# Two k loads moved ahead of DMA transposes, and two weight subtractions moved from VectorE to GpSimd, in a fused attention and maxout kernel

## Chip, cores and metric

The kernel runs on one core of a Trainium2 chip. The metric is device time in microseconds (us) of one execution, the median of several runs; a profiled execution gives the trace. Engines are written as in the profile: PE (TensorE; PEld is its weight loads), DVE (VectorE), ACT (ScalarE), POOL (GpSimd), SP (SyncE, which here issues nearly all DMAs; "SPq" is its queue).

## What is computed

Soft-capped attention over 8 batches of 12 heads (448 positions of 64 elements), then a layer of two first matrices with a maximum between them:

```python
scores = scale * np.matmul(q, k.transpose(0, 1, 3, 2))
scores = cap * np.tanh(scores / cap)
scores = scores - np.max(scores, axis=-1, keepdims=True)
attn = np.exp(scores)
attn = attn / (np.sum(attn, axis=-1, keepdims=True) + 1e-09)
...
h1 = x @ w1                # x: 3584 x 768, the heads side by side
h2 = x @ w2
g = np.maximum(h1, h2)
return (g @ w_out).astype(np.float32)
```

The kernel uses max(h1, h2) = h2 + relu(h1 - h2). It subtracts w2 from w1 once (wd_sb, eight 128-column blocks of x @ (w1 - w2) go through a relu), and multiplies w2 by w_out once (wm_sb), so the output is x @ wm + relu(x @ wd) @ w_out.

## The kernel before

**Units.** Two heads are a pair; there are 48 pairs, 6 in a batch. A group is 3 pairs (L = 3), numbered from 0 in the code, so that there are groups 0 to 15. A step t is 2 pairs (NQ = 24 steps): step t uses pairs 2t and 2t + 1, and pair i belongs to group i // 3. So group 4 is first used by pair 12, the scores of step 6, part 0, and group 5 by pair 15, the scores of step 7, part 1.

**Way of a group.** `load` (L117) issues from SP the DMAs of k, q or v of a group into f32 tiles `kr`, `qr`, `vr`, two buffers each, so a load of group g needs the casts of group g - 2 to be done. From group 2 on a load of k is three DMAs (main, L129, 576 KB, and two of the left-over rows, L142, 48 KB each), one of q two (L129, 576 KB, and L136, 96 KB), one of v three like k. `cast` (L147) turns them to bf16 on POOL: k in L185 and two of L197, q in L185 and L190, v in L164 and two of L169. `cross` (L290) then issues one DMA transpose from SP (L292), from `kqf` to `qkT`, for groups from 2 on; groups 0 and 1 are transposed by PE (`transposes`, L273). `scores` (L302) multiplies from `qkT` (L318, or L315 for the left-over rows of both pairs, part 2) and applies tanh on ACT (L319), out of two `s` buffers and one `v` buffer of PSUM; `ex` (L321) exponentiates on ACT (L324). `add` (L331) sums exponentials on DVE from step 4 on (`esum`, L342 to L346), `total` (L352) makes the row sums and their inverse, `values` (L373) multiplies with v (L381, L387), `normalize` (L400, DVE) writes `xT`.

**Filler.** `moe(b)` (L406) is a generator of the matmuls of one batch: blocks f = 0 to 7 of six matmuls each (L414) with a relu on DVE (L419), then output tiles (L429, L432) with a copy on DVE (L435) and DMAs out. Two PSUM buffers (`mm`) alternate. `F(n)` (L460) emits the next n matmuls of the oldest generator, so PE's order is written out by hand: scores, filler, scores, filler, row sums, values. What is left at the end is emitted at once (L697).

**Weights.** `load_w1` (L228) loads w1 in chunks c = 0 to 5 and halves (columns 0 to 511 and 512 to 1023); `subtract(c, half, engine)` (L234, L236) makes wd_sb. Chunks 0 to 3 lie in tiles named `osb`, 4 and 5 in one named `xT`. The second halves are needed by the blocks f = 4 to 7 of `moe(0)`.

**Order.** Every engine works through its own instructions in the order in which the program emits them, and SP likewise: an issue that has to wait for a semaphore holds up all that are behind it. The schedule is a list written out by hand (L505 to L648) and a loop over the steps from 3 on (L650). `todo[i]` holds loads that `extra(i)` (L494) issues in step i // 2, `crosses[t]` the group that step t transposes (before `extra(2t)`), `casts[t]` the casts at the end of step t, held back by a small copy to `mark` on POOL (L691) that waits for the inverse of that step. Groups from 4 on are planned by L485 to L492; here the lists that matter are todo[4] = k and q of group 4, todo[6] = k and q of group 5, todo[8] = v of group 4, todo[5] empty, crosses[4] = 4, crosses[5] = 5, and casts[3] (moved ahead of the loop, L627) and casts[4] = k and q of groups 4 and 5. L647 moves group 5's loads from step 3 to step 4, behind the transposes of group 4.

Of the kernel before, what the change touches and what calls it, by code (L numbers as in the profile page):

```python
# [10 lines left out]
def kernel(  # L11
# [11 lines left out]
    nc = tc.nc  # L23
# [75 lines left out]
    def half(b):  # L99
        return slice(0, 64) if b % 2 == 0 else slice(64, P)  # L100

    def rows(t, b, h0, h1):

        return t[b, h0:h1, :, :].rearrange("h (r j) d -> (h r) (j d)", j=R7)
# [4 lines left out]
    def raw_of(g, what):  # L109
        if (g, what) not in raw:  # L110
            raw[g, what] = raw_tile(what)
        t = raw[g, what]
        m = t[:, : 2 * L * NJ * D].rearrange("p (h c) -> p h c", c=NJ * D)
        l = t[:, 2 * L * NJ * D :].rearrange("p (h d) -> p h d", d=D)
        return t, m, l

    def load(g, what, n0=0, n1=L, parts=("main", "left")):  # L117
        b, p = divmod(g * L, NP)
        h0, h1 = 2 * (p + n0), 2 * (p + n1)
        src = {"k": k, "q": q, "v": v}[what]  # L120
        t, m, l = raw_of(g, what)
        if g < NT:
            nc.sync.dma_start(
                out=t[:, n0 * S : n1 * S].rearrange("p (n c) -> p n c", c=S),
                in_=rows(src, b, h0, h1).rearrange("(n p) c -> p n c", p=P),
            )
            return
        if "main" in parts:
            nc.sync.dma_start(  # L129
                out=m[:, 2 * n0 : 2 * n1, :],  # L130
                in_=src[b, h0:h1, 0 : NJ * P, :].rearrange("h (p j) d -> p h (j d)", j=NJ),
            )
        if "left" not in parts:
            return
        if what == "q":
            nc.sync.dma_start(  # L136
                out=l[half(b), 2 * n0 : 2 * n1, :],
                in_=src[b, h0:h1, NJ * P : S, :].rearrange("h p d -> p h d"),
            )
        else:  # L140
            for par in range(2):
                nc.sync.dma_start(  # L142
                    out=l[64 * par : 64 * par + 64, n0:n1, :],
                    in_=src[b, h0 + par : h1 : 2, NJ * P : S, :].rearrange("h p d -> p h d"),
                )
# [88 lines left out]
    def subtract(c, part, eng):  # L234
        cs = slice(part * (DF // 2), (part + 1) * (DF // 2))
        eng.tensor_sub(wd_sb[:, c, cs], w1_in[c][:, cs], w2b[part][:, c, :])  # L236
# [31 lines left out]
    def qkT_of(g):  # L268
        if g not in qkT:
            qkT[g] = stage.tile([P, L, 8, P], bf16, name="qkT")  # L270
        return qkT[g]
# [18 lines left out]
    def cross(g, n0=0, n1=L):  # L290

        nc.sync.dma_start_transpose(  # L292
            out=qkT_of(g)[:, n0:n1].rearrange("p n j c -> p (n j) c"),
            in_=kqf[g % 2][:, n0:n1].rearrange("p n j c -> p (n j c)"),
        )
# [6 lines left out]
    def scores(t, p, last=None, js=None):  # L302

        if (t, p) not in tanh:
            tanh[t, p] = att.tile([P, 2 * NJ, S], bf16, name="tanh")
        for j in js or range(NJ if p < 2 else 1):
            s = two_banks(last if last and j == NJ - 1 else s_psum)
            for m in range(2):
                i = 2 * t + (p if p < 2 else m)
                g = i // L  # L310
                k0 = qkT[g][:, i % L, :, :].rearrange("p j c -> p (j c)")
                o = Q0 + (64 * (i // NP % 2) if g >= NT else 0)
                qTn = k0[:, o : o + S]
                if p == 2:
                    nc.tensor.matmul(s[:, m, :S], k0[:, 3 * P : 4 * P], qTn)  # L315
                else:
                    r = slice(64 * m, 64 * m + 64)
                    nc.tensor.matmul(s[:, m, :S], k0[r, j * P : (j + 1) * P], qTn[r, :])  # L318
            nc.scalar.activation(tanh[t, p][:, 2 * j : 2 * j + 2, :], s[:, :, :S], AF.Tanh, scale=scale / cap)  # L319

    def ex(t, p):  # L321
        n = 2 * NJ if p < 2 else 2
        expo[t, p] = att.tile([P, n, S], bf16, name=f"expo{p}", bufs=2)
        nc.scalar.activation(expo[t, p], tanh[t, p][:, 0:n, :], AF.Exp, scale=float(cap))  # L324
# [6 lines left out]
    def add(t, ab, step):  # L331

        if t < NS or t >= NQ:
            return
        if t not in esum:
            esum[t] = att.tile([P, 4, S], bf16, name="esum")
        d = esum[t][:, 2 * ab : 2 * ab + 2, :]
        if step == 2:

            r = slice(64 * ab, 64 * ab + 64)  # L340
            d = esum[t][r, ab::2, :]
            nc.vector.tensor_add(d, d, expo[t, 2][r, :, :])  # L342
        elif step == 0:
            nc.vector.tensor_add(d, e_of(t, ab, 0), e_of(t, ab, 1))  # L344
        else:
            nc.vector.tensor_add(d, d, e_of(t, ab, 2))  # L346
# [5 lines left out]
    def total(t):  # L352

        ss = two_banks(s_psum)[:, 0, :]
        if t < NS:
            for j in range(NJ):
                for ab, h, r in HEADS:
                    nc.tensor.matmul(
                        ss[r, :S], ones[:, :32], e_of(t, ab, j)[:, h, :], start=(j == 0), stop=False
                    )  # L360
            for ab, h, r in HEADS:
                nc.tensor.matmul(ss[r, :S], ones2[:, h, :32], expo[t, 2][:, ab, :], start=False, stop=True)
        else:
            for ab, h, r in HEADS:
                nc.tensor.matmul(ss[r, :S], ones[:, :32], esum[t][:, 2 * ab + h, :], start=True, stop=True)  # L365
        st = att.tile([P, NB, 32], f32, name="st", bufs=1)
        nc.vector.transpose(st.rearrange("p b c -> p (b c)"), ss[:, :S])  # L367
        rs = att.tile([P, NB, 1], f32, name="rs", bufs=2)
        nc.vector.reciprocal(rs, st[:, :, 0:1])
        inv[t] = att.tile([P, S], f32, name="inv", bufs=2)  # L370
        nc.vector.transpose(inv[t].rearrange("p (b c) -> p b c", c=32), rs.to_broadcast([P, NB, 32]))  # L371
# [28 lines left out]
    def normalize(t, ps):  # L400
        for u in range(2):
            nc.vector.tensor_mul(x_of(t, u), ps[:, u, :S], inv[t])  # L402
# [57 lines left out]
    def F(n):  # L460
        rate[1] += n * rate[0]
        while rate[1] >= 1 and fill_q:
            g = fill_q[0]
            if g is not rate[2]:
                rate[2] = g
                next(g)
            rate[1] -= 1
            try:
                next(g)
            except StopIteration:  # L470
                fill_q.pop(0)
        if not fill_q:
            rate[1] = 0.0
# [4 lines left out]
    todo = [[] for _ in range(N)]  # L478
# [15 lines left out]
    def extra(i):  # L494
        for f, a in todo[i]:
            f(*a)
# [56 lines left out]
    def cast_kq(g, n0, n1):  # L553
        for what in ("k", "q"):
            cast(nc.gpsimd, g, what, n0, n1)
# [46 lines left out]
    total(0)  # L602
    transposes(5)
    cast_kq(3, 0, 1)
    for c in range(3):
        subtract(c, 1, nc.gpsimd)
    F(8)
    scores(2, 1, js=(0, 1))
# [8 lines left out]
    load_mains(3, 1, 3)  # L617
    load(2, "v")
    cast_kq(3, 1, 3)
    cross(3, 1, 3)  # L620
    extra(4)
    extra(5)
    load(3, "v")
    total(1)
    normalize(1, values(1))
# [18 lines left out]
    scores(3, 2)  # L644
    ex(3, 1)
    F(14)
    todo[8] = todo[6] + todo[8]  # L647
    todo[6] = []  # L648

    for t in range(3, NQ):  # L650
        i = 2 * t
        more = t + 1 < NQ
        if more:
            scores(t + 1, 0, v_psum)
        ex(t, 2)
        if t == 3:
            subtract(3, 1, nc.vector)
        F(6)
        if t in crosses:
            cross(crosses[t])  # L660
        if t == 3:
            subtract(4, 1, nc.vector)
            cast(nc.gpsimd, 3, "v")
        extra(i)
        F(2)
        add(t, 0, 0)
        F(3)
        if t == 3:
            subtract(5, 1, nc.vector)
        add(t, 0, 1)  # L670
        F(3)
        add(t, 1, 0)
        F(2)
        if more:
            scores(t + 1, 1, v_psum)
            ex(t + 1, 0)
        F(3)
        add(t, 1, 1)
        F(7)
        add(t, 0, 2)  # L680
        F(4)
        add(t, 1, 2)
        extra(i + 1)
        F(8)
        if more:
            scores(t + 1, 2)
            ex(t + 1, 1)
        total(t)
        normalize(t, values(t))
        if casts[t]:  # L690
            nc.gpsimd.tensor_copy(mark, inv[t][:1, :1])  # L691
            for g, what in casts[t]:
                cast(nc.gpsimd, g, what)
        if t % 3 == 2:
            fill_q.append(moe(t // 3))
        F(9)
# [34 lines left out]
```

## Time and profile before

| what | value |
|---|---|
| median of 4 runs | 340.93 us (340.53 to 341.13) |
| profiled execution: its own time, its span | 343.09 us, 340.8 us |
| PE busy | 325.2 us, 95% |
| ACT busy | 278.3 us, 82% |
| DVE, POOL busy | 232.1 us (68%), 111.6 us (33%) |
| chain that ended last, by engine | PE 71%, DMA 15%, POOL 4%, SPq 4%, DVE 3% |
| DMA | 61.78 MB, 181 GB/s over the span |

The span goes from the first to the last instruction; all positions below are us from its start. A line of a timeline gives start, duration, engine, source line, operation, output <- inputs with partitions x elements, and how often in a row; in square brackets stand how long the engine was idle just before it and what ended that. The ends of matmuls are modelled. SP's issues count as the time in which SP was busy issuing, not that of the transfer.

### The profile page before, as it was taken

The numbers are of one execution on the slowest core, as the hardware profiler recorded it, in microseconds if no ns is written. First come the engines' busy times: TensorE is split into PE (matmuls) and PEld (weight loads), VectorE is DVE, ScalarE is ACT, GpSimd is POOL, SyncE is SP. The second block draws the span as 40 slices with busy tenths as digits, with TensorE's granted clock in tenths as the row PEclk, the third lists the DMA queues.
The fourth block names the chain that finished last, engine by engine and source line by source line (L and its number), as shares of the span: only waits on it lengthen the run. The fifth ranks groups of instructions, "written<-read, shape, count | busy, mean of one in ns | idle before, by whom it ended". The sixth has DMA issues, their size and how long they took to land.

```text
span 340.8 us, 6876 instructions
## 1 busy us (share of the span) xinstructions
PE 325.2 (95%) x2722; PEld 163.7 (48%) x2722; DVE 232.1 (68%) x416; ACT 278.3 (82%) x243; POOL 111.6 (33%) x194
## 2 busy tenths in 40 slices
PE   4899998989899999999999999999999999999995
PEld 2555443444444554455445544445445554555563
DVE  5446966597687678776787668776776767874321
ACT  4999999897989999899989999899989999900000
POOL 8345685272424404412421441243144130000000
PEclk9999999999999999999999999999999999999999
DMA  7999999859999999577967599749955920012022
GB/s 227 188 238 273 293 252 272 191 146 230 221 238 280 214 224 288 141 160 157 306 174 160 94 241 312 160 136 236 291 117 147 220 83 15 0 48 92 2 92 92
DMA packets 106239, 61.78 MB, mean 181 GB/s; under 512 B 62816, under 2 KB 101216, under 8 KB 106208
## 3 DMA queue, kind: packets, MB, share of 16 engines
q1 hardware_dynamic: 102336, 58.21, 67.3%
q0 software_dynamic: 3872, 3.15, 6.0%
q8 instruction: 21, 0.34, 0.4%
q14 instruction: 10, 0.08, 0.1%
HBM read 42.47 MB, written 11.01 MB: 157 GB/s over the span
## 4 chain that ended last, share of the span: by engine, by line
PE 71%; DMA 15%; POOL 4%; SPq 4%; DVE 3%; issue 2%; POOLq 0%; DVEq 0%
PE mm L432 20%; PE mm L414 18%; PE mm L429 15%; DMA vr<-in_v_dram 6%; PE v L381 6%; PE s L318 5%; DMA kr<-in_moe_w_out_dram 2%; DMA gT<-in_moe_w_dram 2%; PE s L315 2%; DMA qkT<-kqf 2%; PE v L318 2%; PE v L387 2%; DMA xT<-in_moe_w_dram 2%; PE s L365 2%; DMA osb<-in_moe_w_dram 1%
## 5 line engine op out<-in xcount | busy, mean ns | idle before, releaser
L324 ACT ACTIVATE expo<-tanh 128x2688 bf16<-128x2688 bf16 (+1 forms) x72 | 140.3, 1950 | 0.2
L319 ACT ACTIVATE tanh<-s 128x896 bf16<-128x896 f32 x123 | 107.4, 915 | 16.6 <-PE s L318 13.3
L432 PE MATMUL mm<-wo_sb,gT 128*128 128x384 bf16 x448 | 85.8, 327 | 0.0
L414 PE MATMUL mm<-xT,wd_sb 128*128 128x448 bf16 x384 | 78.2, 353 | 2.2 <-DVE gT L419 1.9
L429 PE MATMUL mm<-wm_sb,xT 128*128 128x384 bf16 x336 | 66.1, 327 | 0.0
L435 DVE COPY osb<-mm 128x384 f32<-128x384 f32 x56 | 31.1, 555 | 44.9 <-PE mm L432 44.5
L432 PEld LDWEIGHTS <-gT 128*128 128x128 bf16 x448 | 42.4, 98 | 34.4 <-issue 8.2
L414 PEld LDWEIGHTS <-wd_sb 128*128 128x128 bf16 x384 | 35.9, 98 | 40.6 <-issue 10.0
L419 DVE TENSOR_SCALAR gT<-mm 128x448 bf16<-128x448 f32 x64 | 39.5, 622 | 18.8 <-PE mm L414 18.6
L429 PEld LDWEIGHTS <-xT 128*128 128x128 bf16 x336 | 31.6, 98 | 26.2 <-issue 6.5
L319 ACT ACTIVATE tanh<-v 128x896 bf16<-128x896 f32 x45 | 41.5, 923 | 0.0
L691 POOL COPY mark<-inv 1x1 f32<-1x1 f32 x17 | 3.0, 177 | 115.8 <-DVE inv L371 92.5
L381 PE MATMUL v<-expo,vp 128*32 128x448 bf16 x576 | 36.0, 353 | 0.0
L318 PE MATMUL s<-qkT 64*128 64x448 bf16 x198 | 28.5, 363 | 2.9 <-DVE qkT L288 1.5
L402 DVE TENSOR_TENSOR xT<-v,inv 128x448 bf16<-128x448 f32 x48 | 27.8, 620 | 2.6 <-PE v L387 0.3
L342 DVE TENSOR_TENSOR esum<-esum,expo 64x896 bf16<-64x896 bf16 x40 | 27.1, 677 | 1.2
L367 DVE STREAM_TRANSPOSE st<-s 128x448 f32<-128x448 f32 x24 | 15.6, 650 | 16.5 <-PE s L365 12.5
L346 DVE TENSOR_TENSOR esum<-esum,expo 128x896 bf16<-128x896 bf16 x40 | 26.2, 654 | 0.8
L344 DVE TENSOR_TENSOR esum<-expo 128x896 bf16<-128x896 bf16 x40 | 26.2, 656 | 0.0
L318 PEld LDWEIGHTS <-qkT 64*128 64x128 bf16 x288 | 10.4, 95 | 25.0 <-issue 16.3
L185 POOL CAST kqf<-kr 128x1152 bf16<-128x1152 f32 (+2 forms) x17 | 16.6, 976 | 14.3 <-DMA kr<-in_k_dram 14.3
L381 PEld LDWEIGHTS <-vp 128*32 128x32 bf16 x576 | 15.6, 97 | 10.2 <-DVE vl L161 0.4
(68 smaller groups left out, 267.1 us busy)
## 6 DMA issues: line engine op xcount, KB each, us to landing
vr<-in_v_dram SPq DMA_DIRECT2D x14, 576.0 KB, 5.0
out_dram<-osb SPq DMA_DIRECT2D x20, 384.0 KB, 4.0
kr<-in_k_dram SPq DMA_DIRECT2D x12, 576.0 KB, 6.8
qr<-in_q_dram SPq DMA_DIRECT2D x12, 576.0 KB, 7.5
out_dram<-osb SPq DMA_DIRECT2D x16, 192.0 KB, 3.7
osb<-in_moe_w_dram SPq DMA_DIRECT2D x8, 256.0 KB, 5.0
gT<-in_moe_w_dram POOLq DMA_DIRECT2D x12, 128.0 KB, 9.5
wo_sb<-in_moe_w_out_dram POOLq DMA_DIRECT2D x4, 384.0 KB, 8.9
```

The costliest lines, as they stand in the source:

```text
L318: nc.tensor.matmul(s[:, m, :S], k0[r, j * P : (j + 1) * P], qTn[r, :])
L319: nc.scalar.activation(tanh[t, p][:, 2 * j : 2 * j + 2, :], s[:, :, :S], AF.Tanh, scale=scale / cap)
L324: nc.scalar.activation(expo[t, p], tanh[t, p][:, 0:n, :], AF.Exp, scale=float(cap))
L342: nc.vector.tensor_add(d, d, expo[t, 2][r, :, :])
L344: nc.vector.tensor_add(d, e_of(t, ab, 0), e_of(t, ab, 1))
L381: nc.tensor.matmul(ps[r, :S], vp[g % 2][:, 2 * n + h, j, u::2], e_of(t, ab, j)[:, h, :], start=(j == 0), stop=False,)
L402: nc.vector.tensor_mul(x_of(t, u), ps[:, u, :S], inv[t])
L414: nc.tensor.matmul(ps[:, :S], wd_sb[:, c, f * P : (f + 1) * P], x[:, c, cs], start=(c == 0), stop=(c == KC - 1))
L419: nc.vector.tensor_relu(g[f // FH][:, f % FH, cs], ps[:, :S])
L429: nc.tensor.matmul(ps[:, : DM // 2], x[:, c, ts], wm_sb[:, c, hs], start=(c == 0), stop=False)
L432: nc.tensor.matmul(ps[:, : DM // 2], g[f // FH][:, f % FH, ts], wo_sb[:, f, hs], start=False, stop=(f == FC - 1))
L435: nc.vector.tensor_copy(osb[:, hs], ps[:, : DM // 2])
```

## The change

Of the six second-half subtractions, five are now on POOL ahead of step 3's loop, where three were; chunks 3 and 4 leave DVE, chunk 5 stays there. The load of k of group 4 is issued in front of the transposes of group 3 (its pairs 1 and 2), that of q behind them; the load of v of group 3 still follows. Of group 5, the load of k goes back to step 3, so that it is issued behind v of group 3 and in front of the transposes of group 4; q stays behind them, in step 4. (A count of groups from 1, instead of the code's from 0, makes these loads those of groups 5 and 6 and the transposes those of groups 4 and 5.)

```diff
@@ -602,7 +602,7 @@
     total(0)
     transposes(5)
     cast_kq(3, 0, 1)
-    for c in range(3):
+    for c in range(5):
         subtract(c, 1, nc.gpsimd)
     F(8)
     scores(2, 1, js=(0, 1))
@@ -617,9 +617,9 @@
     load_mains(3, 1, 3)
     load(2, "v")
     cast_kq(3, 1, 3)
+    load(4, "k")
     cross(3, 1, 3)
-    extra(4)
-    extra(5)
+    load(4, "q")
     load(3, "v")
     total(1)
     normalize(1, values(1))
@@ -644,8 +644,8 @@
     scores(3, 2)
     ex(3, 1)
     F(14)
-    todo[8] = todo[6] + todo[8]
-    todo[6] = []
+    todo[8] = todo[6][1:] + todo[8]
+    todo[6] = todo[6][:1]
 
     for t in range(3, NQ):
         i = 2 * t
@@ -653,13 +653,10 @@
         if more:
             scores(t + 1, 0, v_psum)
         ex(t, 2)
-        if t == 3:
-            subtract(3, 1, nc.vector)
         F(6)
         if t in crosses:
             cross(crosses[t])
         if t == 3:
-            subtract(4, 1, nc.vector)
             cast(nc.gpsimd, 3, "v")
         extra(i)
         F(2)
```

## The prediction

> **What bounds the kernel now.** I read the page's busy shares, then busy time by stage, then the timelines of the single engines around the edited lines. [...]TensorE's clock is granted in full in every slice, so no part of the sum hangs on it. Busy time by stage (length, then busy us of PE, weight loads, DVE, ACT, POOL; clock, DMA share, GB/s):
>
> ```profile
> 52.90:58.40 5.50, 4.29 (x28) 1.69 (x22) 4.29 (x6) 5.21 (x6) 2.92 (x3) 1.00 1.13 239
> 58.40:67.00 8.60, 8.60 (x83) 4.26 (x82) 5.19 (x9) 7.91 (x6) 3.61 (x8) 1.00 0.86 202
> 67.00:80.50 13.50, 11.93 (x98) 6.05 (x97) 11.24 (x16) 11.49 (x10) 7.21 (x9) 1.00 0.74 167
> 80.50:96.50 16.00, 14.67 (x109) 6.74 (x109) 11.22 (x21) 14.86 (x14) 5.71 (x9) 1.00 1.03 228
> 96.50:141.00 44.50, 44.10 (x365) 21.67 (x366) 33.69 (x60) 42.57 (x36) 15.64 (x26) 1.00 1.01 250
> 141.00:293.00 152.00, 151.62 (x1216) 74.28 (x1216) 112.85 (x202) 145.52 (x128) 43.54 (x73) 1.00 0.68 170
> ```
>
> From 96.5 to 293 us PE idles 0.4 of 44.5 and 0.4 of 152 us: what comes earlier at 96.5 is passed on to the end. Ahead of that it idles 1.2, 1.6 and 1.3 us in the first, third and fourth stretch, 4.1 us together: the most that this change can win. ACT stands close behind (14.86 of 16.00). PE's timeline names the places:
>
> ```profile
> 56.12 1.67 PE L414 MATMUL mm<-xT,wd_sb 128*128 128x448 bf16 x8 [1.21 <-DVE gT L419]
> ...
> 76.53 0.37 PE L365 MATMUL s<-esum,ones 128*32 128x448 bf16 x3 [1.05 <-DVE esum L342]
> ...
> 80.52 0.55 PE L318 MATMUL s<-qkT 64*128 64x448 bf16 x4 [0.53 <-DMA qkT<-kqf]
> ...
> 96.57 0.55 PE L318 MATMUL s<-qkT 64*128 64x448 bf16 x4 [0.52 <-DMA qkT<-kqf]
> ```
>
> The first is a PSUM buffer of the MoE filler, late because DVE sat in front of its relu. The third and fourth are transposes landing late: of group 4 (first used at 80.52) and group 5 (96.57). DVE, then POOL, then SP's queue:
>
> ```profile
> 54.05 1.49 DVE L236 TENSOR_TENSOR wd_sb<-osb,gT 128x512 bf16<-128x512 f32 x1 [1.47 <-DMA osb<-in_moe_w_dram]
> 55.46 0.61 DVE L419 TENSOR_SCALAR gT<-mm 128x448 bf16<-128x448 f32 x1
> ```
>
> ```profile
> 52.72 2.27 POOL L236 TENSOR_TENSOR wd_sb<-osb,gT 128x512 bf16<-128x512 f32 x2 [1.08 <-DMA osb<-in_moe_w_dram]
> 57.57 0.92 POOL L185 CAST kqf<-kr 128x768 bf16<-128x768 f32 x1 [2.58 <-DMA kr<-in_k_dram]
> ...
> 69.77 1.15 POOL L185 CAST kqf<-kr 128x1152 bf16<-128x1152 f32 x1 [7.11 <-DMA kr<-in_k_dram]
> ...
> 72.45 1.63 POOL L185 CAST kqf<-qr 128x1152 bf16<-128x1152 f32 x1 [0.17 <-DMA qr<-in_q_dram]
> ```
>
> ```profile
> 60.45 1.95 SPq L292 DMA_TRANSPOSE qkT<-kqf  x1
> 62.44 0.99 SPq L129 DMA_DIRECT2D kr<-in_k_dram  x1
> ...
> 64.80 0.60 SPq L129 DMA_DIRECT2D qr<-in_q_dram  x1
> ...
> 74.94 3.64 SPq L292 DMA_TRANSPOSE qkT<-kqf  x1
> ...
> 90.06 4.51 SPq L292 DMA_TRANSPOSE qkT<-kqf  x1
> ```
>
> SP finishes issuing at 56.5, then stands until 60.45 for POOL's casts of group 3; all of group 4's loads stand behind that. It stands again from 70.4 to 74.94 for group 4's casts, with group 5's loads behind; DMA moves 45 and 3 GB/s in 72 to 74 and 74 to 76.
>
> **Part 1: two subtractions from DVE to POOL.** Removed from DVE: the wait of 1.47 for w1's chunk 3, its subtraction of 1.49, and one of 0.67 (chunk 4). The relu of 55.46 then runs when its matmuls end, about 53.6, done by 54.3; PE's 8 matmuls start at 54.9 (end of the 8 before) and not at 56.12. The next scores need two s buffers (ACT's tanh of 54.57 and 55.4 frees them by 56.3) and the v buffer, freed by the tanh of 56.18 at 57.10. So PE resumes filler at 57.10 + 0.35 = 57.45 and not at 58.41: gain **0.96**, not 1.21.
>
> Added to POOL: 2 of 1.15 us, between 54.99 and its next cast at 57.57, which waits 2.58 us for a DMA. Chunk 4's data have landed by 55.3, so POOL runs to 57.29 and delays nothing, with 0.28 us to spare. Behind it stand the casts of group 3 and SP's transposes of them. A rule speaks against this move: the Trainium skill, "GPSIMD Engine Reference", section 4.1, gives elementwise two-input work to VectorE, GpSimd being about 2 times slower. The rows say 1.15 against 0.67 us, 1.7 times. By the rule the pair takes 2.7 us and overruns the gap by 0.1; by the rows it fits. I take the rows: cost 0. Upper bound: DVE's 1.49 beside POOL's subtractions shows a collision costing 0.8; a pair stretched so is 0.5 late, and the transposes with it. It is not below nothing, since the casts still wait for the same DMA. The filler's fifth block, the first to use the second half of wd_sb, needs chunk 3 at about 57.7 (ready 56.2) and chunk 4 at 57.9 (ready 57.3): no wait, with 0.6 us to spare. Chunk 5 stays on DVE.
>
> **Part 2: load of k, group 4, ahead of the transposes of group 3.** Three issues, 0.99 + 1.27 = 2.26 us, go into SP's stand at 56.5 and end at 58.8, ahead of 60.45: no cost to SP while POOL's casts hold it there, up to 2.26 us if they did not. Its buffer was read for the last time at 48.7: no wait. q's group 4 then follows the transposes at 62.4, not 64.8, and v's group 3 likewise: 2.4 us earlier. The bytes are the price: 576 + 2 x 48 = 672 KB at 246 GB/s (62 to 72) is 2.8 us of DMA, in a stretch full until 60 and nearly empty (0.26) until 62. The Trainium skill, "DMA: Bandwidth & Descriptors", section "Queues, rings and completion order", says that each DMA engine consumes one queue's descriptors in ring order, which speaks against both loads here: by that, whatever of k is left stands wholly ahead of the transposes. Before, these landed 4.3 us after issue, at 64.75, and the scores start at 67.00. By the rule at worst 64.75 + 2.8 = 67.5; by the rows, 6.5 us to landing at 90.06 behind v and outputs against 5.5 at 74.94 with nothing ahead, +1.0: 65.8. I take 65.8, since k's load has two nearly empty us to drain in. With part 1 the scores want them at 66.04: cost 0, bounds 0 and 1.5.
>
> **Part 3: group 4's transposes.** k is cast before q comes. q lands 7.5 us after issue as before: 69.9 and not 72.3. Casts of q (before 1.63 and 0.89, ending 74.9) end between 71.6 and 72.4. Transposes: +5.5 as at 74.94, so 77.5; k of group 5, now issued behind v at 68 to 70.4 (in SP's second stand, with 1.2 us to spare; its buffer was last read at 59.1), puts its 2.8 us ahead of them. In ring order from 65.8 come q, v, k at 2.8 each, to 74.2, and then 4 us of transposes (the 76 to 80 stretch): about 78.6. By the rows' +1.0: 78.5. The two agree; without backlog 77.1, with one twice as long 80.
>
> PE's own side: from 66.04, 11.93 us of work, plus the DVE wait at 76.53 of 0 to 1.05: 77.97 to 79.02. That wait comes from esum additions that took 1.56 (one) and 3.31 us (two) beside POOL's casts, against 0.65 for one alone; with k's casts gone from that stage some collisions go, q's and v's remain. I take the middle. ACT: the gaps at 58.20 and 67.47 shrink with PE, and from 66.5 its 11.5 us end at 78.0. The latest of the three: PE's scores at about 78.8, not 80.52: gain **1.72**, part 1 included.
>
> **Part 4: group 5.** k, landed by 75, is cast at once when POOL's gate opens (before: 4.58 us of waiting). q goes out behind the transposes of group 4, about 76 and not 80.58, v of group 4 behind it; q's casts end near 83.5 and not 90.03. Transposes are out by 84 to 86 and land by 92. The scores of 96.57 want them at 94.3: the 0.52 goes. ACT has 15.0 us between these two tanh, PE 15.5: PE sets it. Gain **0.5**.
>
> **Sum.** 1.72 + 0.52 = 2.24, say 2.3 us with the parts rounded. Behind, group 6's transposes landed at 115.1 for scores at 116.80; their gate is a DVE result of the same stage, and their loads go out earlier, so they move along. The profiled execution took 343.09 (span 340.8 and 2.3 around it): I expect a span of 338.5, an execution of 340.8. The median of runs, 340.93, is 2.2 below the profiled one for the same work: 340.93 - 2.3 = **338.6**.
>
> **Rivals.**
> A (0.60), as worked out, with group 4's scores between 78.0 and 79.6: gain 1.4 to 3.0, 337.9 to 339.5.
> B (0.15), the DVE wait at 76.53 goes entirely and transposes come in 77.1: PE and ACT both allow 78.0, and 0.5 + 0.2 behind it: gain 3.2 to 3.7, 337.2 to 337.7. For it: two of six casts leave the stage. Against: q's and v's are the later ones.
> C (0.15), a wait takes the place of the removed one: the k loads take back ahead of the transposes what the early issue gives, and group 4's land at 80 as before. Then part 1's gain ends in a longer wait there; left are 0.5 to 0.9: 340.2. For it: DMA is full from 62 to 72. Against: it is empty from 72 to 76.
> D (0.10), slower: k of group 5 shares the engines with q of group 4, which lands at 72.3 as before, or later; casts end at 74.9 and the transposes need 6.5, not 5.5: 81.4. It decides as soon as they are issued after about 74.5: then the scores lose 0.9, more than the 0.5 left at 96.57. Price 0.4 to 1.2: 341.7.
>
> Two runs of this kernel can be told apart from about 0.2% (0.7 us). Faster by more than that: A, B and nearly half of C, 0.82; the rest of C and a little of D, 0.09; slower, 0.09. For 8 in 10 the range goes from B's lower end to C's middle: 337.2 to 340.4.
>
> **What would show it.** Right: no DMA wait in DVE's L236 near 54; POOL's second pair done by 57.6; transposes of group 3 landed before their scores (no wait at 66); group 4's issued near 72; no DMA wait of PE at group 5's first scores, which start near 94.3; idle unchanged behind. Wrong: PE waiting for qkT at 66, group 4's transposes issued later than 74, an esum wait over 1 us, or ACT gaps kept while PE's shrink.

## The result, and the profile after

| | before | after |
|---|---|---|
| median of runs | 341.59 us (63 runs, 339.59 to 343.18) | 340.56 us (44 runs, 339.33 to 342.59) |
| profiled execution, span | 343.09, 340.8 us | 341.72, 339.8 us |

The ratio is 0.9973, 95% interval 0.9963 to 0.9983: the change wins 0.9 us (0.6 to 1.3) of 341.6. Forecast were 2.3 us and 338.6 (337.2 to 340.4). The direction is right, the size is less than half of it, and 340.56 lies above the range. The 63 runs also put the kernel before 0.7 us higher than the four runs that I had.

For every run of the changed kernel, and for the runs of before that were timed beside the experiments below, the span is on record too. It divides the gain into two parts of about equal size. The span of the changed kernel is 338.65 us in the median of its 44 runs; that of the kernel before is 339.2 us in the median of those 124 runs. So about 0.55 us of the gain lie in the span. The time outside the span (a run's time less its span) went from 2.39 us (2.19 to 2.55) to 1.93 us (1.73 to 2.07), two ranges that do not touch: 0.45 us more, which the forecast did not have.

The same six stretches of the changed kernel, columns as before:

```profile
52.90:58.40 5.50, 5.32 (x32) 2.11 (x30) 2.63 (x5) 5.47 (x5) 5.49 (x5) 1.00 1.12 260
58.40:67.00 8.60, 8.04 (x80) 4.07 (x79) 5.04 (x9) 8.13 (x7) 6.65 (x12) 1.00 1.06 251
67.00:80.50 13.50, 13.12 (x109) 7.05 (x108) 10.71 (x17) 12.22 (x11) 6.37 (x9) 1.00 1.01 231
80.50:96.50 16.00, 14.88 (x111) 6.81 (x110) 12.13 (x19) 15.06 (x16) 6.26 (x9) 1.00 1.04 254
96.50:141.00 44.50, 43.99 (x365) 21.37 (x363) 33.50 (x60) 42.03 (x36) 14.18 (x25) 1.00 0.85 218
141.00:293.00 152.00, 151.74 (x1230) 74.50 (x1232) 113.02 (x201) 146.36 (x129) 42.53 (x72) 1.00 0.68 169
```

PE's idle time shrank in the first stretch (1.2 to 0.2 us) and the third (1.6 to 0.4), and a new 0.6 appeared in the second. DMA's share in the second and third rose from 0.86 and 0.74 to 1.06 and 1.01: the holes were filled. PE's timeline says what the new 0.6 and the rest are:

```profile
59.04 3.96 PE L414 MATMUL mm<-xT,wd_sb 128*128 128x448 bf16 x20 [0.56 <-POOL wd_sb L236]
...
67.70 0.55 PE L318 MATMUL s<-qkT 64*128 64x448 bf16 x4 [0.38 <-DMA qkT<-kqf]
...
79.30 0.55 PE L318 MATMUL s<-qkT 64*128 64x448 bf16 x4
...
95.09 0.55 PE L318 MATMUL s<-qkT 64*128 64x448 bf16 x4
```

The waits at the scores of groups 4 and 5 (before at 80.52 and 96.57) are gone. New are two: for chunk 4 on POOL, and for the transposes of group 3 at 67.70, which I had at 66.04 without a wait. On DVE both relus wait for their own matmuls only, as forecast; POOL is what came late, then SP:

```profile
54.29 0.62 DVE L419 TENSOR_SCALAR gT<-mm 128x448 bf16<-128x448 f32 x1 [1.23 <-PE mm L414]
55.42 0.62 DVE L419 TENSOR_SCALAR gT<-mm 128x448 bf16<-128x448 f32 x1 [0.51 <-PE mm L414]
```

```profile
52.91 4.96 POOL L236 TENSOR_TENSOR wd_sb<-osb,gT 128x512 bf16<-128x512 f32 x4 [2.37 <-DMA osb<-in_moe_w_dram]
57.83 1.15 POOL L236 TENSOR_TENSOR wd_sb<-xT,gT 128x512 bf16<-128x512 f32 x1
58.93 0.82 POOL L185 CAST kqf<-kr 128x768 bf16<-128x768 f32 x1
...
70.97 1.19 POOL L185 CAST kqf<-qr 128x1152 bf16<-128x1152 f32 x1 [5.24 <-DMA qr<-in_q_dram]
```

```profile
57.33 0.60 SPq L129 DMA_DIRECT2D kr<-in_k_dram  x1
...
61.71 2.89 SPq L292 DMA_TRANSPOSE qkT<-kqf  x1
64.64 0.58 SPq L129 DMA_DIRECT2D qr<-in_q_dram  x1
...
73.02 4.26 SPq L292 DMA_TRANSPOSE qkT<-kqf  x1
...
84.76 4.48 SPq L292 DMA_TRANSPOSE qkT<-kqf  x1
```

w1's chunk 0 landed 2.4 us later than in the trace of before (POOL starts at 52.91; 50.49 there), so POOL's five subtractions ended at 58.98 and not at 57.29. Group 4's transposes went out at 73.02 (74.94), group 5's at 84.76 (90.06).

From this one trace I took theory P: POOL's extra work and the k load in front of the transposes each take back part of the gain. Rival K: the k load alone takes it back. A third: ACT caps what can be won. After the first runs a fourth came up, V: the trace of before had waits that most executions do not have.

### The profile page after: what moved, and what is told of

Same layout as the page of the kernel before. It is cut to its first block, busy times and chain, and to the rows that moved or that the text cites. A ratio compares the mean times of both kernels' runs of the same rounds, so it can differ in the third digit from the quotient of the medians.

```text
span 339.8 us, 6879 instructions
## 1 busy us (share of the span) xinstructions
PE 325.2 (96%) x2722; PEld 164.2 (48%) x2722; DVE 229.7 (68%) x414; ACT 278.4 (82%) x243; POOL 112.8 (33%) x196
## 4 chain that ended last, share of the span: by engine, by line
PE 81%; DMA 8%; DVE 6%; ACT 1%; SPq 1%; POOL 1%; issue 1%; DVEq 0%; POOLq 0%; ACTq 0%
PE mm L432 22%; PE mm L414 17%; PE mm L429 16%; PE v L381 7%; PE s L318 6%; DMA wo_sb<-in_moe_w_out_dram 5%; PE mm L256 3%; PE s L315 2%; PE v L387 2%; PE v L318 2%; PE s L365 2%; DMA qkT<-kqf 2%; DMA vr<-in_v_dram 1%; DVE gT L419 1%; ACT tanh L319 1%; DVE esum L344 1%
## 5 line engine op out<-in xcount | busy, mean ns | idle before, releaser
L344 DVE TENSOR_TENSOR esum<-expo 128x896 bf16<-128x896 bf16 x40 | 27.6, 690 | 0.0
L342 DVE TENSOR_TENSOR esum<-esum,expo 64x896 bf16<-64x896 bf16 x40 | 25.5, 637 | 1.2
L185 POOL CAST kqf<-qr 128x1152 bf16<-128x1152 f32 (+2 forms) x17 | 16.6, 979 | 8.9 <-DMA qr<-in_q_dram 8.0
```

## Experiments

All ratios are to the kernel before on the same chip, with 95% intervals. Positions drift by up to 1.7 us between executions (the row sums of step 1, PE's L358, start between 46.26 and 47.97), so the scores are given as the distance from these row sums. "PE idle" is the sum of PE's waits from 3 to 52 us behind them. A span is that of the traced execution.

| kernel | ratio | step 5, part 0 | step 6, part 0 | step 7, part 1 | PE idle | span |
|---|---|---|---|---|---|---|
| before, three traces | | 20.27, 20.13, 19.62 | 33.79, 33.58, 32.49 | 49.84, 49.05, 48.15 | 4.12, 2.86, 2.35 | 340.8, 340.3, 340.3 |
| after, four traces | 0.9973 | 20.50, 20.19, 19.77, 19.32 | 32.10, 31.71, 31.35, 30.82 | 47.89, 47.55, 46.82, 46.29 | 2.03, 1.88, 1.44, 1.05 | 339.8, 339.1, 338.6, 338.5 |
| e1 subtractions only | 0.9999 | 19.32 | 32.17 | 47.63 | 1.52 | 339.1 |
| e2 loads only | 0.9979 | 19.57 | 31.08 | 46.54 | 1.00 | 338.7 |
| e3 k of group 4 behind | 0.9993 | 19.32 | 32.20 | 47.93 | 2.21 | 339.0 |
| e4 chunk 4 on DVE | 0.9960 | 19.41 | 30.91 | 46.37 | 1.05 | 338.4 |
| e5 chunks 3, 4 on DVE, later | 0.9963 | 19.96 | 31.46 | 46.92 | 1.56 | 337.8 |
| e7 k and q of group 4 in front | 1.0089 | 21.92 | 35.10 | 50.57 | 3.59 | 342.5 |
| e8 k of group 5 behind | 0.9958 | 19.32 | 30.82 | 46.53 | 1.18 | 338.2 |
| e9 as e4, pair-wise transposes | 0.9947 | 19.32 | 30.82 | 46.71 | 1.07 | 337.8 |
| e10 as e4, k of group 5 behind | 0.9964 | 19.68 | 31.18 | 47.06 | 1.52 | 337.9 |
| e11 before, only k of group 4 in front | 0.9965 | 19.32 | 30.85 | 46.45 | 1.19 | 337.8 |
| e12 as e9, k of group 5 behind | 0.9957 | 19.32 | 30.82 | 46.37 | 1.13 | 337.5 |

### Single halves: e1, e2

```diff
 # e1: the kernel before, with
-    for c in range(3):
+    for c in range(5):
         subtract(c, 1, nc.gpsimd)
...
-        if t == 3:
-            subtract(3, 1, nc.vector)
...
-            subtract(4, 1, nc.vector)
```

> Only the two subtractions move to POOL; all loads stand as before. Theory P (POOL's pair and the k load in front of the transposes each take back part of the gain): PE's wait of 1.2 us for the relu goes, but POOL ends chunk 4 about 1 us later than I reckoned, PE waits 0.3 to 0.6 us for it at the fifth filler block, and the transposes of group 3 are issued 0.5 to 1 us later than before. They land 4.3 us after issue, since nothing stands in front, so the scores of step 5 start 0.2 to 0.5 us earlier than before, measured from the scores of step 4. Rival K (the k load alone takes it back): no wait for chunk 4, those scores 0.9 us earlier. Both: group 4's transposes land when they did, so PE's gain ends in a longer wait there; total 0 to 0.5 us faster, ratio 0.9985 to 1.000.

Measured: 0.9999 (0.9981 to 1.0016), no gain. The relu's wait is gone and there is none for chunk 4, so the scores of step 5 come at 19.32, 0.3 to 0.95 us earlier than in the three traces of before. PE (then ACT, then SP) of e1:

```profile
66.35 0.55 PE L318 MATMUL s<-qkT 64*128 64x448 bf16 x4
...
75.76 0.74 PE L381 MATMUL v<-expo,vp 128*32 128x448 bf16 x10 [0.47 <-POOL vp L164]
...
79.20 0.55 PE L318 MATMUL s<-qkT 64*128 64x448 bf16 x4
```

```profile
79.66 1.73 ACT L319 ACTIVATE tanh<-s 128x896 bf16<-128x896 f32 x2 [1.30 <-PE s L318]
```

```profile
73.59 3.64 SPq L292 DMA_TRANSPOSE qkT<-kqf  x1
```

From step 5 to step 6 PE needs 12.85 us here, as in the third trace of before (12.87), against 11.5 in the kernels that load k early. The one wait listed in that stretch is 0.47 us for v on POOL; PE lists none for group 4's transposes, which land 5.6 us after issue, at 79.2, just as PE arrives; ACT runs dry for 1.3 us. This trace is still ahead of all three of before at step 6 (32.17 against 32.49 to 33.79), so it does not show how typical runs come to gain nothing. The runs' spans show two parts that cancel: the time outside the span fell from 2.39 to 1.94 us, and the span is 339.60 us in the median of 14 runs, 339.20 before, a difference within their spread (their means are 339.45 and 339.34).

e2 is the other half: the loads of the change, subtractions as before (its diff is the second and third part of the change's).

> Only the loads move; chunks 3 and 4 stay on DVE in their old places. Theory P: the wait of 1.2 us at the relu stays, but POOL casts group 3 as early as before; its transposes land some 6 us after issue behind the k load, near the point at which PE wants them, wait at most 0.3 us. Behind it the waits for esum (1.05) and for the transposes of groups 4 and 5 (0.5 each) go as in the changed kernel: total 1.3 to 2.1 us faster than before, ratio 0.994 to 0.996, that is better than the whole change. Rival K: the transposes of group 3 hold PE for 0.7 us or more, total at most 0.9 us, ratio 0.997 or more. Third theory (ACT sets a ceiling on what can be won): the same ratio as the whole change, 0.997, with ACT gapless from step 4 to step 7.

Measured: 0.9979 (0.9966 to 0.9993). The ratio lies above what P gave (0.994 to 0.996) and nearer to the other two; the trace, with 11.5 us from step 5 to step 6, looks like P. Unexpected: the wait of 1.2 us at the relu is not in its trace, although DVE, which keeps the subtractions here, waits 0.99 us for w1's chunk 3.

### Single parts of the change undone: e3, e4, e8

The diffs of e3, e4, e8, e5 and e7 are against the changed kernel.

```diff
 # e3
-    load(4, "k")
     cross(3, 1, 3)
+    load(4, "k")
     load(4, "q")
```

> The whole change, but with k of group 4 loaded behind the transposes of group 3, right ahead of q. Theory P: these transposes land 4.3 us after issue again and not 5.9, so the scores of step 5 don't wait for them and start 0.4 us earlier than in the changed kernel; group 4's q comes no later than with k in front, since its place in the queue of bytes is the same, but it is issued 2.3 us later, so group 4's transposes go out 1 to 2 us later than in the changed kernel and hold PE for up to 1 us. Total 0 to 1 us slower than the whole change: ratio to before 0.997 to 1.000. Rival K: 0.7 to 1 us faster than the whole change, ratio 0.994 to 0.995.

Measured: 0.9993 (0.9976 to 1.0010), as P had it. Group 3's transposes land 4.6 us after issue, no wait at step 5; then PE's lines of step 5 and 6:

```profile
65.58 0.55 PE L318 MATMUL s<-qkT 64*128 64x448 bf16 x4
...
78.46 0.55 PE L318 MATMUL s<-qkT 64*128 64x448 bf16 x4 [0.36 <-DMA qkT<-kqf]
```

12.88 us between them, with the wait for group 4 back (and 0.46 us for v on POOL). K, by which this kernel had to be faster, falls.

```diff
 # e4
-    for c in range(5):
+    for c in range(4):
         subtract(c, 1, nc.gpsimd)
...
         if t == 3:
+            subtract(4, 1, nc.vector)
             cast(nc.gpsimd, 3, "v")
```

> The whole change, but chunk 4's second half is subtracted on DVE in its old place behind the first relu; POOL keeps chunks 0 to 3. Theory P: POOL is free 1.15 us earlier, PE's wait of 0.56 us for chunk 4 goes, the transposes of group 3 are issued about 1.1 us earlier and the scores of step 5 start 0.7 to 1.1 us earlier than in the changed kernel. Total 0.7 to 1.1 us faster than the whole change, ratio to before 0.994 to 0.9955. Rival K: the transposes still land 5.9 us after issue and PE's own work in front sets the rest; 0 to 0.3 us faster than the whole change, ratio 0.9965 to 0.9975. ACT ceiling: no difference, 0.997.

Measured: 0.9960 (0.9945 to 0.9975). The point lies between P's 0.9955 and K's 0.9965, and the interval overlaps with that of the whole change, so it does not decide between them.

```diff
 # e8
-    todo[8] = todo[6][1:] + todo[8]
-    todo[6] = todo[6][:1]
+    todo[8] = todo[6] + todo[8]
+    todo[6] = []
```

> The whole change without the early load of k of group 5, which goes back behind the transposes of group 4. The wait for group 5's transposes that this load was to take away showed in one of three traces of before only, so I expect no difference from the whole change, 0.9965 to 0.998, with group 4's transposes landing 5.5 us after issue instead of 5.7, and at most 0.3 us of waiting at group 5's scores. If the early k of group 5 carries the gain: 0.5 us or more slower than the whole change, 0.9985 to 1.000.

Measured: 0.9958 (0.9941 to 0.9974): nothing is lost without the early k of group 5. Its transposes land at 91.3 us, 2.4 us ahead of their scores (93.74).

### The same kernels profiled again

No edit; two traces each.

> The kernel before, unchanged, profiled once more. Theory S (the waits that I read are the kernel's own): PE waits 1.2 us for the relu near 55, about 1 us for esum in step 4 and 0.5 us each for the transposes of groups 4 and 5, all within 0.3 us, and the span is within 0.5 us of 340.8. Theory V (the profiled execution, 1.5 us above the median of 63 runs, had waits that most executions don't have): at least one of the first two waits is shorter by over 0.5 us, and the span is 338.5 to 340.0.

> The kernel before, profiled a third time; as for the second. If S holds, all three traces agree in the four waits within 0.3 us; if V holds, the two new ones lie nearer to the median of runs than the first and PE's idle time from 50 to 98 us is 1 to 2 us smaller than the 4.2 us of the first.

> The changed kernel, profiled once more. Theory P (POOL and the k load in front take gain back, in every execution): PE waits 0.4 to 0.7 us for chunk 4 on POOL and 0.2 to 0.5 us for the transposes of group 3; the scores of step 5 start 20.5 us behind the row sums of step 1, as in the first trace. If the two waits were that execution's own: neither over 0.2 us, and the scores of step 5 start 19.4 us behind.

> The changed kernel, profiled a third time; as for the second. P: both waits again in at least one of the two new traces, together over 0.5 us; otherwise they are chance.

Before, second and third trace, PE:

```profile
55.86 1.29 PE L414 MATMUL mm<-xT,wd_sb 128*128 128x448 bf16 x6 [0.64 <-DVE gT L419]
57.42 0.54 PE L414 MATMUL mm<-xT,wd_sb 128*128 128x448 bf16 x2 [0.27 <-DVE gT L419]
...
76.57 0.75 PE L381 MATMUL v<-expo,vp 128*32 128x448 bf16 x10 [0.47 <-POOL vp L164]
...
80.62 0.55 PE L318 MATMUL s<-qkT 64*128 64x448 bf16 x4 [0.67 <-DMA qkT<-kqf]
...
96.09 0.55 PE L318 MATMUL s<-qkT 64*128 64x448 bf16 x4
```

```profile
56.10 1.67 PE L414 MATMUL mm<-xT,wd_sb 128*128 128x448 bf16 x8 [0.56 <-DVE gT L419]
...
76.30 0.37 PE L365 MATMUL s<-esum,ones 128*32 128x448 bf16 x3 [0.85 <-DVE esum L342]
...
79.84 0.55 PE L318 MATMUL s<-qkT 64*128 64x448 bf16 x4
...
95.50 0.55 PE L318 MATMUL s<-qkT 64*128 64x448 bf16 x4
```

Of the four waits that I had read, the relu's is 1.21, 0.91, 0.56 us; that of step 4's end 1.05, 0.47 (then for v on POOL), 0.85; group 4's transposes 0.53, 0.67, none; group 5's 0.52, none, none. Together 3.31, 2.05 and 1.41 us. S, which wanted all within 0.3, falls. V has the shorter waits right, but the two spans (340.3) came out above its 338.5 to 340.0: these are not the typical executions either.

The changed kernel's third trace, PE:

```profile
67.02 0.55 PE L318 MATMUL s<-qkT 64*128 64x448 bf16 x4 [0.38 <-DMA qkT<-kqf]
...
78.60 0.55 PE L318 MATMUL s<-qkT 64*128 64x448 bf16 x4
...
94.07 0.55 PE L318 MATMUL s<-qkT 64*128 64x448 bf16 x4
```

The wait for group 3's transposes stands in three of four traces of the change (0.38, 0.53, 0.38, none); the wait of 0.56 for chunk 4 was that of the first trace alone. But POOL still cost something in the second trace. Its POOL:

```profile
56.58 1.60 POOL L236 TENSOR_TENSOR wd_sb<-xT,gT 128x512 bf16<-128x512 f32 x1
58.12 0.82 POOL L185 CAST kqf<-kr 128x768 bf16<-128x768 f32 x1
```

k of group 3 had landed at 57.5 there and was cast 0.6 us later, behind chunk 4; in the first trace it had landed at 58.2 and was cast at 58.93. In the third and fourth POOL waited for k. So the first half of P (POOL) holds in two of four traces, the second (k in front) in three.

### Two ways around the late transposes, and the price doubled: e5, e9, e7

```diff
 # e5
-    for c in range(5):
+    for c in range(3):
         subtract(c, 1, nc.gpsimd)
...
         if t == 3:                       # behind F(6) and its relu
+            subtract(3, 1, nc.vector)
+            subtract(4, 1, nc.vector)
             cast(nc.gpsimd, 3, "v")
```

> All loads as in the changed kernel, but POOL keeps only chunks 0 to 2, and DVE subtracts chunks 3 and 4 one after the other behind the first relu of step 3, so that the relu is not held. Theory P: the wait at the relu goes as in the changed kernel, POOL is free 2.3 us earlier and casts group 3 when its k lands; its transposes are issued 0.3 to 1 us earlier and land 6.1 us later, behind the k load: PE waits 0.2 us or less for them. 0.2 to 0.8 us faster than the whole change, ratio to before 0.995 to 0.9965, as with chunk 4 alone on DVE. If POOL was no cost: as the whole change, 0.997.

Measured: 0.9963 (0.9944 to 0.9982). POOL is free when group 3's k lands (57.5) and casts it at 57.60, and PE still waits 0.57 us for group 3's transposes, which land 6.3 us after issue: here it is not POOL that makes them late.

```diff
 # e9: as e4, and
-    cast_kq(3, 1, 3)
+    cast_kq(3, 1, 2)
+    cast_kq(3, 2, 3)
     load(4, "k")
-    cross(3, 1, 3)
+    cross(3, 1, 2)
+    cross(3, 2, 3)
```

> The whole change with chunk 4 on DVE, and the casts and transposes of group 3's pairs 1 and 2 cut into one pair each, k of group 4 still in front. The scores of step 5, part 0, need only pair 1. Theory P: its transposes are issued about 1 us earlier, after half the casts, and have half the bytes, so they land by 65.5; no wait for them, PE then held only by ACT. 0 to 0.5 us faster than with chunk 4 on DVE alone, ratio to before 0.994 to 0.996. Against it: one more issue of 1.25 us on SP and four more casts on POOL, which put the loads of q behind by 0.5 us or so; if that weighs more, 0.9965 to 0.998.

Measured: 0.9947 (0.9929 to 0.9966), the lowest point of all; the first pair's transposes land 4.4 us after issue and the wait is gone. It is faster than before; against the change itself the intervals overlap.

```diff
 # e7
     load(4, "k")
-    cross(3, 1, 3)
     load(4, "q")
+    cross(3, 1, 3)
```

> The whole change, with q of group 4 in front of the transposes of group 3 too: 1344 KB instead of 672 KB stand ahead of them, to double the suspected price. If one queue's transfers go by in the order of issue, these transposes land 8 to 9 us after issue (4.6 with nothing ahead, 6.1 with k), at 69 to 70; PE waits 2 to 3 us for them at the scores of step 5, and the total is 0 to 1 us slower than before, ratio 1.000 to 1.003. If the engines share themselves among the transfers, 6.5 to 7 us, wait under 1 us and a total as in the whole change or better, 0.996 to 0.998, since group 4's casts come earlier.

Measured: 1.0089 (1.0061 to 1.0116), 3.0 us slower. The landing is as the ring order has it, 8.2 us after issue (4.3 to 5.1 in three traces of before, 6.1 on average in the first three of the change), with a wait of 2.54 us. But the total went far past the expectation of 1.003. PE, and the windows around it (PEclk is the third column from the right):

```profile
69.39 0.55 PE L318 MATMUL s<-qkT 64*128 64x448 bf16 x4 [2.54 <-DMA qkT<-kqf]
...
74.45 0.55 PE L318 MATMUL s<-qkT 64*128 64x448 bf16 x4
```

```profile
66.00:69.30 3.30, 0.86 (x6) 0.29 (x3) 0.69 (x2) 0.85 (x1) 1.29 (x2) 1.00 1.05 177
70.50:73.50 3.00, 3.00 (x11) 1.35 (x10) 1.67 (x3) 2.73 (x4) 2.00 (x3) 0.50 1.18 281
74.00:78.00 4.00, 4.00 (x28) 2.09 (x26) 2.46 (x5) 3.08 (x4) 0.00 (x0) 1.00 1.03 228
```

About 1 us behind the wait TensorE's granted clock fell to 0.50, for 3.4 us, and was 1.00 again from 74: the way to the next scores took 5.06 us, 3.38 in the changed kernel (67.70 to 71.08), 1.7 us on top of the wait. The mean granted clock is 0.990 to 0.995 in eight of the ten runs of e7 and 1.00 in two, so that this came in most of its executions, but not in all.

### What carries the gain: a4, e10, e11, e12

> The changed kernel itself, timed beside the next three on one chip. Ratio to before 0.9965 to 0.998, as in its 44 runs.

> The whole change, with chunk 4 on DVE and k of group 5 behind the transposes of group 4. If chunk 4 on POOL and the early k of group 5 each cost some of the gain, 0.3 to 0.7 us faster than the whole change on the same chip, ratio 0.9945 to 0.9965. If k of group 5 carries gain, slower than with chunk 4 on DVE alone (0.996): 0.997 to 0.999. If neither does anything: 0.9965 to 0.998, as the whole change.

> The kernel before with one thing changed: k of group 4 is loaded in front of the transposes of group 3. Its q and v of group 3 move up by that. If this carries most of the gain: the wait for group 4's transposes goes, those of group 3 land 6 us after issue, the relu's wait stays; ratio 0.9965 to 0.9985. If it only helps with the rest of the change: 0.9985 to 1.001.

> Chunk 4 on DVE, pair-wise casts and transposes of group 3, and k of group 5 behind. The wait for group 3's transposes is gone already with the pairs (0.9947 with k of group 5 in front), so this differs from that by k of group 5 alone: if it does nothing, 0.994 to 0.9955; if it gains, 0.996 to 0.9975; if it costs, 0.993 or less.

e10 is e4 with e8's edit, e12 is e9 with it, a4 the change itself. e11 is the kernel before with

```diff
+    load(4, "k")
     cross(3, 1, 3)
-    extra(4)
-    extra(5)
+    load(4, "q")
```

Measured on one chip: a4 0.9962 (0.9943 to 0.9981), e10 0.9964 (0.9944 to 0.9983), e11 0.9965 (0.9945 to 0.9986), e12 0.9957 (0.9938 to 0.9976). e10 shows no gain over a4, and e12 lies between its two expectations, so that neither gives the early k of group 5 a worth. The one moved load of e11 gives as much in all as the whole change, but not the same part: its span is 0.9 us shorter than before (338.2 against 339.1 in the median) and its time outside the span is as before (2.37 against 2.40 us), where the change has 0.55 us from each (338.55 and 1.85). Two expectations for e11 were missed: the relu's wait is not in its trace, and group 3's transposes land 4.4 us after issue. PE, then SP, of e11:

```profile
66.52 0.55 PE L318 MATMUL s<-qkT 64*128 64x448 bf16 x4
...
78.05 0.55 PE L318 MATMUL s<-qkT 64*128 64x448 bf16 x4
...
93.65 0.55 PE L318 MATMUL s<-qkT 64*128 64x448 bf16 x4
```

```profile
55.26 0.60 SPq L129 DMA_DIRECT2D kr<-in_k_dram  x1
55.90 1.84 SPq L142 DMA_DIRECT2D kr<-in_k_dram  x2
59.28 3.08 SPq L292 DMA_TRANSPOSE qkT<-kqf  x1
62.40 0.59 SPq L129 DMA_DIRECT2D qr<-in_q_dram  x1
...
71.17 3.64 SPq L292 DMA_TRANSPOSE qkT<-kqf  x1
```

From step 5 to step 6 PE takes 11.53 us. In all traces with k of group 4 alone in front it is 11.5 to 11.6; before it was 13.52, 13.45 and 12.87; with k back behind, 12.85 (e1) and 12.88 (e3). That is the gain in the span, 1.3 to 2.0 us in these traces; PE's listed waits are 0.5 to 1.6 us of it, and the rest is in no listed wait. Here k in front cost nothing at group 3's transposes (4.4 us to landing, as e8's 4.7 and a4's 4.8), where it cost about 1.5 in the other traces with it (5.9 to 6.3). It is not the bytes alone that decide between the two: the last of k lands ahead of the transposes in all ten traces with k alone in front and pairs 1 and 2 in one transpose, 1.7 to 1.9 us ahead in these three and 3.3 to 3.7 us in the other seven. In those seven DMA's share falls to between 0.41 and 0.80 for a microsecond shortly before the transposes land, so the engines are in part free by then. What holds the transposes up is not settled.

The time outside the span follows one edit, the subtraction of chunk 3. Wherever the span is on record, it is 2.19 to 2.55 us in every run of the four kernels that leave this subtraction on DVE (before, e2, e5, e11) and 1.73 to 2.12 in every run of those that have it on POOL (the change, e1, e3, e4, e7 to e10, e12). e4 and e5, in which DVE has chunk 4 in both and chunk 3 in e5 alone, stand at 1.93 and 2.38. No trace shows what lies in that time, so why the edit shortens it is open.

## Why the prediction was wrong in size

**What failed: the last line of the sum.** I took waits out of the one profiled execution, 343.09 us, and subtracted their worth from the median of runs, 340.93, "for the same work". The work was the same, the waits were not. In three traces of before the four waits come to 3.31, 2.05 and 1.41 us, and the first, the largest, was mine; that execution was 1.5 us above the median of 63 runs, and its span of 340.8 us was 1.6 us above the median span of before (339.2). Waits that one execution has and the typical one has not cannot be taken from the median. The 2.3 us were to come out of the span; the median span gave 0.55. Within the traced executions the forecast does better, but is not reached: the span was to be 338.5, and four of the change have 339.8, 339.1, 338.6 and 338.5 (mean 339.0; before 340.8, 340.3, 340.3). That the mean of their times, 340.97, is near the 340.8 that I expected is in part luck, since 0.3 to 0.4 us of it come from the time outside the span, which I had left at 2.3. Against the mean of the three traces of before (342.79) the change wins 1.8 us, against the medians of runs 0.9 (0.6 to 1.3), on the later chip 0.9962, 1.3 us. All three profiled executions of before lie above its median, by 0.9 to 1.5; on the chip of the second and third a further run took 342.63 us, so the chip may have a part in this. That typical executions have still shorter waits than these three is what the times suggest; no trace here shows one.

**Part 1, the relu: 0.96 expected; by itself it gave nothing in the span.** The mechanism is right (the wait goes; DVE waits for its matmuls only), and against my trace so is the size: e1 has step 5's scores at 19.32 and not 20.27. But that was one execution's: the wait is 1.21, 0.91, 0.56 us in the three traces, none in e2 and e11, which keep the subtractions on DVE. It depends on when w1's chunk 3 lands and on how long its subtraction then takes (1.49, 0.92, 0.69 us in the three). The median span of e1 shows nothing of it. What this part did give is the 0.45 us outside the span, of which the sum had nothing. POOL's cost of 0 was right in two of four traces: in two POOL cast group 3 0.6 to 0.7 us late, and in one of these PE waited 0.56 us for chunk 4. In that one w1's chunk 0 landed 2.4 us later than in my trace; the collision behind my upper bound of 0.5 was the smaller part (4.96 us for four subtractions of 1.15).

**Part 2, k ahead of group 3's transposes: cost 0 expected, 0.4 us of waiting in three of four traces.** The scores of step 5 were to start 19.3 us behind the row sums (66.04 less 46.73); they started at 20.50, 20.19, 19.77 and 19.32. Ring order was the better guide than the row that I preferred in most traces: 8.2 us to landing with 1344 KB in front, 5.9 to 6.3 with 672 in seven traces, 4.3 to 5.1 (mean 4.7) with none. In the three other traces with 672 KB the landing took 4.4 to 4.8 us and my cost of 0 held, so the order of the bytes is not the whole of it. I took +1.0, and the landing (64.8, 67.1, 65.8 in three traces of before) varies by as much.

**Part 3, group 4's transposes: 78.8 expected, 79.30, 78.57, 78.60 and 78.48 measured.** Near, by errors that cancel: step 5 started later than reckoned in three of the four, but the stretch behind it took 11.5 us and not 12.76. The wait at 76.53, which I halved, went altogether, and PE's way is 11.5 us in the traces without a wait, where I had taken its busy time of 11.93 from a trace with waits. There is a slip in the sum too: my own terms end at 78.0 (ACT), 78.5 (PE) and 78.6 at most (transposes; 74.2 and 4 are 78.2), and I took 78.8. k is cast ahead of step 4's additions, and what is left of POOL's casts (L342 for two: 2.13 and 2.06 us in the first two traces of the change, 1.3 in the others, 3.31 in mine of before) no longer makes PE wait. Group 4's transposes landed at 78.8 to 77.0, against 79.8 to 80.5.

**Part 4, group 5: 0.5 expected, nothing.** Its transposes do land earlier (89.3 to 90.8 us, mean 90.2, against 94.8 to 96.6, mean 95.5). But the wait for them was in one of three traces of before, and with group 4's transposes early it is gone without this edit (e8, e10 to e12: 90.7 to 91.8, scores at 93.2 to 93.7).

**The rivals.** 340.56 is near the 340.2 of rival C, but not by its mechanism: no trace of the change has PE waiting for group 4's transposes, and the wait that took back part of the gain stands ahead of them, at group 3's ("PE waiting for qkT at 66" was one of my signs of being wrong). The traces look most like rival B, which had the wait at 76.53 go entirely and the transposes come in by 77.1 (they landed at 77.0 to 78.8); its 3.2 to 3.7 us did not come, for the reason that holds for mine. D's point (issue after 74.5) was not reached: 70.96 to 73.02. An ACT ceiling is not what held the change: its first trace has ACT waiting 1.45 us for PE at 68.16.

**What stays open.** Differences between the variants that keep k of group 4 in front (0.9947 to 0.9979) are smaller than their intervals, so whether pair-wise transposes (e9) beat the change, and whether chunk 4 on POOL or the early k of group 5 cost anything on average, is not decided. Nor is it shown which waits a typical execution of before lacks, nor what lies in the 0.45 us outside the span.

## What to carry to other kernels

A wait read in one trace is a sample: in a stage that runs at DMA's limit profile the kernel before two or three times, and take from a median only the waits that all traces show. If the profiled execution is slower than the runs by as much as the change is to win, the change has to be summed against that execution, and the median credited with less. Compare spans as well as times: here nearly half of the gain lay outside the span, where no reading of the trace could have put it. When loads stand behind an issue that waits, ask for each which consumer it really serves: here one load, moved past one blocked transpose, gave all of the gain in the span that can be measured, and one subtraction moved from DVE to POOL the gain outside it.

## What was not expected of the hardware

A wait of PE of 2.54 us (e7) was followed by a granted clock of 0.50 for 3.4 us, which cost 1.7 us on top of the wait; waits of up to 1.2 us in the other traces left it at 1.00. The landing of the same transposes with the same bytes in front takes 4.4 to 4.8 us in three traces and 5.9 to 6.3 in seven others, although the bytes in front land first in all ten. And the move of one subtraction from DVE to POOL took 0.45 us off the time outside the span.
